# A fused adaLN, attention and MLP kernel: scale, shift and biases made as rows and turned; ScalarE's order by blocks; the second block turned row tile by row tile

## The chip, the core and the metric

The kernel runs on one core of a Trainium2 chip. The metric is the device time of one execution in microseconds (us). The time before is 1591.86 us, the median of three runs from 1589.67 to 1594.28. All times in the text are in us unless marked ns.

The engines are named as in the profile: PE is TensorE (PEld its weight loads), DVE VectorE, ACT ScalarE, POOL GpSimd and SP SyncE, which issues the transfers (DMA). Each engine works through its own list of instructions in order and waits for the others by semaphores. A tile is 128 partitions deep. PE's clock is throttled: the profile shows the clock that was granted, as a share of full speed.

## What is computed

One layer with adaptive layer norm: multi-query attention of 32 heads that share one key and one value head of 16 columns, then an MLP with gelu. All is 32-bit floating point; 2048 rows of 512. Cut to what matters:

```python
mod = (_silu(c) @ w_mod).reshape(c.shape[0], 6, 1, -1)        # c: 1 x 512, w_mod: 512 x 3072
sa, ca, ga, sb, cb, gb = (mod[:, i] for i in range(6))
h = _layernorm(x) * (1 + ca) + sa
q, k, v = h @ wq, h @ wk, h @ wv                              # wq: 512 x 512; wk, wv: 512 x 16
x = x + ga * (softmax(q k^T / 4) v per head) @ wo
h = _layernorm(x) * (1 + cb) + sb
x = x + gb * (gelu(h @ w1 + b1) @ w2 + b2)
```

## The kernel before

The kernel folds the scale `1 + ca` into the weights and turns the shift `sa` into biases: q is (layernorm(x)) times (wq scaled by rows) plus `sa @ wq`, and the keys and values likewise. So before the first product of q it needs the scale as a column (one number for each partition, for each of the four slices of the 512), and before the first q or key leaves PSUM it needs the biases as columns too.

Products that need accuracy are made of three: each operand is split into a high part (rounded) and a low part (the rest), and high by high, low by high and high by low are added up. `split` makes the two parts: the high one on ScalarE or POOL, the low one on VectorE or POOL.

The program has a prologue of some 113 us and then a long regular stretch: 64 units of queries, for each of which PE makes scores (`e`, line 682), ScalarE their exponents, PE the products with the values (`acc`), and VectorE the row maxima (`mx`, line 582) of scores that PE made ahead (`m`, line 577). In that stretch a planner with due times mixes the projections and the MLP in. The change touches the prologue alone; there the order is written out by hand. Every engine's list follows the order of the statements from line 1362 on: what a statement calls goes to the end of each list that it uses.

The rows of x are taken in four blocks of 512 (`xts[0]` to `xts[3]`), each of four row tiles of 128. For a block `stats1` makes mean and variance (VectorE, a power on POOL), `xhat1` normalizes the four row tiles in place (lines 418 and 420; ScalarE, VectorE or POOL), `turn1(b, d)` has PE transpose slice d of the row tiles into one PSUM bank (`tp`, line 428), and `split1(b, d)` splits it: for block 0 a cast on ScalarE and a subtraction on VectorE, for the others a copy on ScalarE (`x`, line 438), a cast on ScalarE (`bigH`, line 140) and a subtraction on POOL (`bigL`, line 145). `keys(b)` makes the 12 products of the block's keys and values (`kps`, line 170), and at the end ScalarE writes the keys (`ks`, line 450); `low_k`, `repeat_k` and `v_out` finish them. `q_group` makes 128 columns of q in 12 products (`qps`). `chunk(n)` is n score products with their maxima, alternating between the two halves of the partitions.

The scale and the shift come from `mod_cols(ps, i, k)`: for slice k of the silu of c it multiplies the 128x128 pieces of `w_mod` (as weights) by one column (`modc`, line 312), 16 products for each of the two. POOL scales the weights of q (`scale_wq`, line 349), and `split_wq` splits them into `wqH` and `wqL` in the order in which the heads are used. The biases of q come from `bias_q` (four products of one column, line 373), `take_col` (a copy on ScalarE, line 377) and `order_q` (a product with the matrix `order`, line 381, that puts the numbers into the heads' order, and a copy on ScalarE). For the first 128 columns this is done ahead, for the other three groups in `prep_wq`, the parts "wq 1" to "wq 3" of the table.

`SLOTS` sets the order of the prologue's later part. Each entry is a slot, and its items are taken from left to right: a number is a `chunk` of so many score products, a name is the next step of that job. "heads b" is `turn1` and `split1` of one slice of block b, "keys b" three key products, "low b" and "k b" the finishing of the keys, "q 1" three products of the second q group, "rows" the four row products of the late modulation (`mod_rows`, `modl`, line 307), which takes the same columns of c 32 times over as weights (`csb`) and data of 512 columns. From slot `WIDE` on, the score products use further banks. `WARM` gives numbers of products that serve nothing but to keep PE busy: `warm_up` at the start, `keep_warm` (`idle`, line 297) elsewhere. After the last slot come nine of these, and then the first scores of the regular stretch.

## Time and profile before

| | |
|---|---|
| runs | 1594.28, 1589.67, 1591.86 us |
| the profiled execution | 1595.28 us, of which the span from the first to the last instruction is 1593.5 us |
| PE busy | 1573.8 us, 99% of the span |
| DVE busy | 1397.7 us, 88% |
| ACT busy | 1230.5 us, 77% |
| POOL busy | 682.1 us, 43% |
| mean granted clock of PE | 0.98 |

How to read the lines that follow. The page cuts the span into 40 equal slices and gives the share of each in tenths. A view by windows has for each window its length, then for each engine its busy time and number of instructions, the granted clock, the share of the DMA engines and the rate. A row of the timeline has start, length, engine, line, operation, output and input tiles, shapes and the number of instructions that follow each other; in brackets stands the idle time ahead of it and what ended it. Such a length runs from the start of the first to the end of the last. A product of unsplit 32-bit operands appears as two instructions of PE, so that 16 such products count as 32; a transpose, or a product of split parts, appears as one. The chain of waits has start, length, engine, tile and line of those pieces that followed from each other up to the last instruction.

### The profile page before, as it was taken

Reading aid. Unit: us, or ns where it says so; the run is one execution under the profiler, and the core shown is the slowest. Engines: PE = TensorE matmul, PEld = TensorE weight load, DVE = VectorE, ACT = ScalarE, POOL = GpSimd, SP = SyncE. Lnnn points to the kernel's source line nnn. Section 1 sums busy time; section 2 is a strip of 40 time slices with the busy share of each in tenths; the row PEclk is TensorE's granted clock in tenths of the full one; section 3 lists DMA queues with packets and bytes.
Section 4 is the critical chain, followed back from the end, with each engine's and each line's share of the span. In section 5 each row is a group of like instructions: output and inputs, shape, how many; then the busy total and the mean of one; then the engine's idle time right before and its main releaser. Section 6 shows DMA issues by size and latency. Waiting matters only on the chain.

```text
span 1593.5 us, 41812 instructions
## 1 busy us (share of the span) xinstructions
PE 1573.8 (99%) x16531; PEld 988.4 (62%) x16531; DVE 1397.7 (88%) x2489; ACT 1230.5 (77%) x2409; POOL 682.1 (43%) x1211
## 2 busy tenths in 40 slices
...
PEclk7679999999999999999999999999999999999999
...
GB/s 207 104 19 121 185 136 45 97 111 60 82 26 103 19 106 33 50 78 56 83 25 103 18 107 32 50 81 49 100 32 76 40 118 26 80 29 98 47 147 47
DMA packets 83976, 120.67 MB, mean 76 GB/s; under 512 B 21294, under 2 KB 56686, under 8 KB 83524
## 3 DMA queue, kind: packets, MB, share of 16 engines
...
q8 instruction: 131, 2.15, 0.6%
...
q10 hardware_dynamic: 16, 0.00, 0.0%
...
## 4 chain that ended last, share of the span: by engine, by line
PE 89%; DVE 8%; DMA 1%; POOL 1%; ACT 1%; SPq 0%; issue 0%; ACTq 0%; DVEq 0%; POOLq 0%
PE acc L703 30%; PE m L577 25%; PE e L682 16%; PE w1ps L203 8%; DVE mx L582 6%; PE w2ps L203 2%; PE w2ps L193 2%; PE w1ps L193 1%; PE kps L170 1%; PE qps L203 1%; PE wops L203 1%; PE tp L203 1%; PE qps L170 0%; PE tp L428 0%; DVE st L888 0%; DMA wml<-in_w_mod_dram 0%
## 5 line engine op out<-in xcount | busy, mean ns | idle before, releaser
L582 DVE TENSOR_REDUCE mx<-m 128x1 f32<-128x512 f32 x2048 | 1270.9, 682 | 113.4 <-PE m L577 92.7
L686 ACT ACTIVATE p<-e 128x512 f32<-128x512 f32 x2048 | 1099.0, 598 | 255.1 <-PE e L682 109.8
L577 PE MATMUL m<-ks,qst 64*128 64x512 f32 x2048 | 838.1, 433 | 5.5 <-DVE ks L454 2.0
L682 PE MATMUL e<-qst,ks 64*128 64x512 f32 x2048 | 740.1, 411 | 0.0
L703 PE MATMUL acc<-p,va 128*32 128x256 f32 x8192 | 548.0, 385 | 0.0
L577 PEld LDWEIGHTS m<-ks,qst 64*128 64x128 f32 x2048 | 368.1, 186 | 209.3 <-DVE mx L582 171.7
L682 PEld LDWEIGHTS e<-qst,ks 64*128 64x128 f32 x2048 | 359.3, 184 | 89.4 <-ACT p L686 62.1
L703 PEld LDWEIGHTS acc<-p,va 128*32 128x32 f32 x8192 | 213.9, 109 | 214.2 <-issue 111.1
L203 PE MATMUL w1ps<-h2H,w1t 64*128 64x256 f32 x1232 | 236.0, 288 | 0.0
L625 POOL TENSOR_SCALAR mt<-turned 8x32 f32<-8x32 f32 x256 | 53.2, 208 | 406.1 <-DVE turned L631 394.2
L203 PEld LDWEIGHTS w1ps<-h2H,w1t 64*128 64x128 f32 x1232 | 185.9, 185 | 29.0 <-issue 21.8
L203 PE MATMUL w1ps<-h2L,w1t 64*128 64x256 f32 x616 | 169.1, 274 | 0.0
L203 PE MATMUL w2ps<-w2H,gH 64*128 64x512 f32 x274 | 120.3, 439 | 0.0
L203 PEld LDWEIGHTS w1ps<-h2L,w1t 64*128 64x128 f32 x616 | 113.9, 185 | 0.0
L203 PE MATMUL w2ps<-w2L,gH 64*128 64x512 f32 x274 | 107.4, 392 | 0.0
L203 PE MATMUL w2ps<-w2H,gL 64*128 64x512 f32 x274 | 106.9, 390 | 0.0
L1040 POOL TENSOR_SCALAR tt<-tt 128x256 f32<-128x256 f32 x77 | 31.0, 403 | 128.4 <-ACT tt L1039 93.5
L1041 POOL TENSOR_TENSOR tt<-tt,z 128x256 f32<-128x256 f32 x77 | 57.0, 740 | 6.4
L145 POOL TENSOR_TENSOR gL<-z,gH 128x256 fp32r<-128x256 f32 x77 | 56.9, 739 | 6.4
L1051 POOL TENSOR_TENSOR z<-tt,z 128x256 f32<-128x256 f32 x77 | 56.4, 732 | 6.0
L1050 POOL TENSOR_TENSOR tt<-tt,z 128x256 f32<-128x256 f32 x77 | 56.9, 739 | 0.0
L203 PEld LDWEIGHTS w2ps<-w2H,gH 64*128 64x128 f32 x274 | 50.4, 184 | 6.7 <-issue 2.9
(216 smaller groups left out, 1573.8 us busy)
## 6 DMA issues: line engine op xcount, KB each, us to landing
...
```

Of the source, the lines that this page charges most:

```text
L145: eng_l.tensor_tensor(out=dst_l, in0=src, in1=raw(dst_h), op=ALU.subtract)
L193: nc.tensor.matmul(ps, a, b_, start=first_, stop=last_)
L203: ins = nc.tensor.matmul(ps, a[rows], b_[rows], start=first_ and s == 0, stop=last_ and s == 1)
L577: nc.tensor.matmul(m, qsts[u][rows, j, t * P:(t + 1) * P], ks[rows, kc * 512:(kc + 1) * 512], start=True, stop=True)
L582: nc.vector.tensor_reduce(out=self.mx[u][:, i, kc:kc + 1], in_=m, axis=AX.X, op=ALU.max)
L625: nc.gpsimd.tensor_scalar(out=mt[:, g:g + 32], in0=turned[g:g + 4 * T, :], scalar1=1.0, scalar2=0.0, op0=ALU.mult, op1=ALU.add)
L682: nc.tensor.matmul(e, ks[rows, kt * P:(kt + 1) * P], rhs, start=True, stop=True)
L686: ins = nc.scalar.activation(dst, e, AF.Exp, scale=0.25)
L703: ins = nc.tensor.matmul(accs[u][32 * cidx:32 * cidx + 32, :], va[:, kt, :], rhs, start=kt == 0, stop=kt == NKT - 1)
L1041: nc.gpsimd.tensor_tensor(out=tt, in0=tt, in1=z, op=ALU.mult)
L1050: nc.gpsimd.tensor_tensor(out=tt, in0=tt, in1=z, op=ALU.mult)
L1051: nc.gpsimd.tensor_tensor(out=z, in0=tt, in1=z, op=ALU.add)
```

## The change

1. *Scale and shift as rows.* `mod_row(ps, i, k)` takes the columns of c, 32 times over, as weights and a 128x512 piece of `w_mod` as data, so that one product replaces four; four of them add up a row of 512 numbers on 32 partitions. ScalarE copies the row from PSUM (`modr`), `turn_rows` transposes its four pieces on PE, and the numbers are read off as columns. For the scale this stands before block 0's turns; for the shift, one row product stands behind each row tile of block 0, and the copy behind the last.
2. *The first weights of q are scaled on ScalarE*, in four instructions, instead of one on POOL.
3. *Biases as rows.* The shift is copied 32 wide (`sab`); `bias_row` multiplies it (as weights) by the unscaled weights of q or of keys and values (as data, 128 columns). ScalarE copies the rows, and puts the heads into order on the way, so that the matrix `order` and its products go; PE turns them. `bias_rest` makes the biases of the other three groups in one go (384 columns of data) in the middle of block 1, and `prep_wq` loses them.
4. *ScalarE's order by blocks.* Blocks 2 and 3 were normalized right behind block 1; now this stands in the slots as "x 2" and "x 3", behind the splits of block 1.
5. *Block 1 is turned row tile by row tile.* Behind each row tile that ScalarE normalizes, PE turns its first three slices and makes two idle products; the fourth slice follows behind the first split. The slots "heads 1" go.
6. `WARM` is (20, 6, 2, 9) for (20, 4, 4, 9); the second number stands once, the third now four times. `WIDE` is 16 for 18, and the slots are laid anew.

The same number of score products is made up to the first exponent; the order of SP's transfers is the same.

```diff
@@ -22,14 +22,13 @@
 LEAD = 6
 LEAD_0 = 6
 FIRST_MAX = ((0, 0), (1, 0), (0, 1), (1, 1), (0, 2), (0, 3), (1, 2), (1, 3))
-SLOTS = (("heads 1", "heads 1"), (2, "heads 1"), (2, "heads 1"),
-         (2, "keys 1"), (2, "keys 1"), (2, "keys 1"), (2, "keys 1"),
-         ("heads 2", "low 1", "k 1", "heads 2"), (2, "heads 2"), (2, "heads 2", "v 0"), (2, "heads 3"),
-         (2, "keys 2"), (2, "keys 2", "heads 3"), (2, "keys 2"), (2, "keys 2"),
-         ("heads 3", "low 2", "k 2", "heads 3"), (2, "wq 1", "keys 3"), (2, "v 1", "keys 3"), (4, "keys 3", "keys 3"),
+SLOTS = ((2, "x 2"), (2, "keys 1"), (2, "keys 1"), (2, "keys 1"), (2, "x 3", "keys 1"),
+         ("heads 2", "low 1", "k 1", "heads 2"), (2, "heads 2"), (2, "heads 2", "v 0"),
+         (2, "heads 3"), (2, "keys 2", "heads 3"), (2, "keys 2"), (2, "keys 2"), (2, "keys 2"), ("heads 3", "low 2", "k 2", "heads 3"),
+         (2, "wq 1", "keys 3"), (2, "v 1", "keys 3"), (4, "keys 3", "keys 3"),
          ("q 1", "low 3", "k 3", "q 1"), (4, "q 1", "v 2", "q 1"), ("wq 2", "v 3"), (4, "rows"),
          (2, "rows"), (2, "rows", "wq 3"), (2, "rows", "load"), (2,))
-WIDE = 18
+WIDE = 16
 MAX_WAIT = (1, 4)
 QBUFS = 4
 PREP = 4
@@ -45,7 +44,7 @@
 SOON = 6
 GROUP = 4
 NORM_WAIT = 6
-WARM = (20, 4, 4, 9)
+WARM = (20, 6, 2, 9)
 MOD_WAIT = 3
 AHEAD = 4.5
 
@@ -306,16 +305,20 @@
         for i, part in enumerate(wm):
             nc.tensor.matmul(ps[32 * i:32 * i + 32, :], csb[:, k, :], part, start=k == 0, stop=k == KD - 1)
 
-    def mod_cols(ps, i, k):
-
-        for d in range(KD):
-            nc.tensor.matmul(ps[:, d:d + 1], wms[k][:, i, d * P:(d + 1) * P], cs[:, k:k + 1], start=k + d == 0, stop=k + d == 2 * KD - 2)
+    def mod_row(ps, i, k):
+
+        nc.tensor.matmul(ps[32 * i:32 * i + 32, :], csb[:, k, :], wms[k][:, i, :], start=k == 0, stop=k == KD - 1)
+
+    def turn_rows(ps, rows, i, n):
+        for k in range(n):
+            nc.tensor.transpose(ps[:, k, :], rows[32 * i:32 * i + 32, k * P:(k + 1) * P], ident[32 * i:32 * i + 32, 32 * i:32 * i + 32])
 
...
     wkL = pro.tile([P, KD, P], F32R, name="wkL")
+    sab = pro.tile([P, KD, 32], F32, name="sab")
     wk0 = pro.tile([P, KD, P], F32, name="wk0")
-    wkm = pro.tile([P, KD, P], F32, name="wkm")
+    wkm = pro.tile([P, KD, P], F32, name="wkm", tag="h32", bufs=4)
...
@@ -328,10 +331,6 @@
...
-
-    order = pro.tile([P, P], F32, name="order")
-    nc.gpsimd.tensor_scalar(out=order.rearrange("p (a r j) -> p a j r", j=2, r=16), in0=ident.rearrange("p (a j r) -> p a j r", j=2, r=16),
-                            scalar1=1.0, scalar2=0.0, op0=ALU.mult, op1=ALU.add)
 
@@ -368,25 +367,29 @@
             nc.scalar.copy(dh, src)
             nc.gpsimd.tensor_tensor(out=dl, in0=src, in1=raw(dh), op=ALU.subtract)
 
-    def bias_q(ps, g):
+    def bias_row(ps, w):
         for k in range(KD):
-            nc.tensor.matmul(ps, wqf[:, k, g * P:(g + 1) * P], sa[:, k:k + 1], start=k == 0, stop=k == KD - 1)
-
-    def take_col(src, g):
-        col = pro.tile([P, 1], F32, name=f"bqn{g}", tag="bqn", bufs=2)
-        nc.scalar.copy(col, src)
-        return col
-
-    def order_q(col, ps, g):
-        nc.tensor.matmul(ps, order, col, start=True, stop=True)
-        nc.scalar.copy(bq[:, g:g + 1], ps)
+            nc.tensor.matmul(ps, sab[:, k, :], w[:, k, :], start=k == 0, stop=k == KD - 1)
+
+    def take_q(dst, ps):
+
+        nc.scalar.copy(dst.rearrange("p (a r j) -> p a j r", j=2, r=16), ps.rearrange("p (a j r) -> p a j r", j=2, r=16))
 
     def prep_wq(g):
         scale_wq(g)
-        ps = psum.tile([P, 2], F32, name=f"bq{g}", **ebank())
-        bias_q(ps[:, 0:1], g)
-        order_q(take_col(ps[:, 0:1], g), ps[:, 1:2], g)
         split_wq(g)
+
+    def bias_rest():
+
+        n = KD - 1
+        ps = psum.tile([P, n * P], F32, name="bqs", tag="x")
+        row = pro.tile([32, n * P], F32, name="bqr", tag="h32", bufs=4)
+        bias_row(ps[:32], wqf[:, :, P:D])
+        for i in range(n):
+            take_q(row[:, i * P:(i + 1) * P], ps[:32, i * P:(i + 1) * P])
+        for i in range(n):
+            nc.tensor.transpose(ps[:, i * P:i * P + 32], row[:, i * P:(i + 1) * P], ident[:32, :32])
+        nc.scalar.copy(bq[:, 1:KD], ps.rearrange("p (i n) -> p i n", n=P)[:, :, 0])
 
     hts = {}
     hts_stats = {}
@@ -1362,35 +1365,45 @@
     warm_up(WARM[0])
     key_rows()
     stats1(0)
-    ps = psum.tile([P, KD], F32, name="modc", tag="x")
+    modr = pro.tile([P, D], F32, name="modr", tag="h32", bufs=4)
+    psr = psum.tile([P, D], F32, name="modrow", tag="x")
+    psc = psum.tile([P, 2, KD, 32], F32, name="modc", tag="v")
     for k in range(KD):
-        mod_cols(ps, 1, k)
-    nc.scalar.activation(ca1, ps, AF.Identity, bias=1.0)
-    scale_wq(0)
-    ps = psum.tile([P, KD], F32, name="modc", tag="v")
+        mod_row(psr, 1, k)
+    nc.scalar.copy(modr[32:64], psr[32:64])
+    turn_rows(psc[:, 1], modr, 1, KD)
+    nc.scalar.activation(ca1, psc[:, 1, :, 0], AF.Identity, bias=1.0)
+    wqms[0] = pro.tile([P, KD, P], F32, name="wqm0", tag="wqm", bufs=1)
+    for k in range(KD):
+        nc.scalar.activation(wqms[0][:, k, :], wqf[:, k, 0:P], AF.Identity, scale=ca1[:, k:k + 1])
     split_wq(0)
     for t, _ in enumerate(xhat1(0, dve)):
         for d in range(KD):
             turn1(0, d, [t])
-        mod_cols(ps, 0, t)
+        mod_row(psr, 0, t)
+    nc.scalar.copy(modr[0:32], psr[0:32])
+    turn_rows(psc[:, 0], modr, 0, KD)
     spread_wkv()
     scaled(wkm, wk0, dve)
     load_constants()
-    nc.vector.tensor_copy(out=sa, in_=ps)
+    nc.vector.tensor_copy(out=sab, in_=psc[:, 0, :, 0:1].to_broadcast([P, KD, 32]))
     for d in range(KD):
         split1(0, d)
     group = q_group()
     run(group, 1)
-    ps = psum.tile([P, 3], F32, name="biases", tag="m", bufs=3)
-    bias_q(ps[:, 1:2], 0)
-    for k in range(KD):
-        nc.tensor.matmul(ps[:, 0:1], wk0[:, k, :], sa[:, k:k + 1], start=k == 0, stop=k == KD - 1)
-    col = take_col(ps[:, 1:2], 0)
+    psb = psum.tile([P, 4, P], F32, name="biases", tag="m", bufs=3)
+    rowb = pro.tile([32, 2, P], F32, name="rowb")
+    bias_row(psb[:32, 0, :], wqf[:, :, 0:P])
+    bias_row(psb[:32, 1, :], wk0)
+    take_q(rowb[:, 0, :], psb[:32, 0, :])
+    nc.scalar.copy(rowb[:, 1, :], psb[:32, 1, :])
     split(wkH, wkL, wkm, act, pool)
-    nc.vector.tensor_copy(out=vbias, in_=ps[:, 0:1])
-    nc.vector.scalar_tensor_tensor(out=kbias, in0=ps[:, 0:1], scalar=kkeep, in1=kmin, op0=ALU.mult, op1=ALU.add)
     run(group, KD - 2)
-    order_q(col, ps[:, 2:3], 0)
+    for i in range(2):
+        nc.tensor.transpose(psb[:, 2 + i, :32], rowb[:, i, :], ident[:32, :32])
+    nc.vector.tensor_copy(out=bq[:, 0:1], in_=psb[:, 2, 0:1])
+    nc.vector.tensor_copy(out=vbias, in_=psb[:, 3, 0:1])
+    nc.vector.scalar_tensor_tensor(out=kbias, in0=psb[:, 3, 0:1], scalar=kkeep, in1=kmin, op0=ALU.mult, op1=ALU.add)
 
     def first_q(t):
         if t == 1:
@@ -1410,17 +1423,24 @@
             repeat_k(0)
 
     stats1(2, first_k)
-    run(xhat1(1, act))
     load_mods(0)
     load_mods(1)
     keep_warm(WARM[1], tag="x", bufs=1)
-    chunk(4)
-    keep_warm(WARM[2], tag="x", bufs=1)
+    for t, _ in enumerate(xhat1(1, act)):
+        if t < 2:
+            chunk(2)
+        for d in range(KD - 1):
+            turn1(1, d, [t])
+        keep_warm(WARM[2], tag="x", bufs=1)
+    split1(1, 0)
+    turn1(1, KD - 1)
+    split1(1, 1)
+    bias_rest()
     stats1(3)
     load_mods(2)
-    run(xhat1(2, act))
-    run(xhat1(3, act, 2))
-    work = {"keys 1": keys(1), "heads 1": heads(1), "heads 2": heads(2), "heads 3": heads(3), "q 1": q_group(), "keys 2": keys(2), "keys 3": keys(3),
+    split1(1, 2)
+    split1(1, 3)
+    work = {"keys 1": keys(1), "x 2": one(run, xhat1(2, act)), "x 3": one(run, xhat1(3, act, 2)), "heads 2": heads(2), "heads 3": heads(3), "q 1": q_group(), "keys 2": keys(2), "keys 3": keys(3),
...
```

How the lists change at the three places of which the prediction speaks. First PE's list at the start, before, from behind `warm_up` to behind the first row tile of block 0 (`modc` is the bank for scale or shift, `wm` a piece of `w_mod`, `tp` a bank of transposes):

```order
L312 MATMUL modc<-cs,wm_133 128x1 x4
L312 MATMUL modc<-cs,wm_134 128x1 x4
L312 MATMUL modc<-cs,wm_135 128x1 x4
L312 MATMUL modc<-cs,wm_136 128x1 x4
L428 MATMUL tp_0_270<-ident,xt_131 128x128
L428 MATMUL tp_1_272<-ident,xt_131 128x128
L428 MATMUL tp_2_274<-ident,xt_131 128x128
L428 MATMUL tp_3_276<-ident,xt_131 128x128
L312 MATMUL modc<-cs,wm_133 128x1 x4
```

and of the change:

```order
L310 MATMUL modrow<-wm_133,csb 32x512
L310 MATMUL modrow<-wm_134,csb 32x512
L310 MATMUL modrow<-wm_135,csb 32x512
L310 MATMUL modrow<-wm_136,csb 32x512
L314 MATMUL modc<-ident,modr 128x32 x4
L431 MATMUL tp_0_266<-ident,xt_131 128x128
L431 MATMUL tp_1_268<-ident,xt_131 128x128
L431 MATMUL tp_2_270<-ident,xt_131 128x128
L431 MATMUL tp_3_272<-ident,xt_131 128x128
L310 MATMUL modrow<-wm_133,csb 32x512
```

Where sixteen products of one column stood (and four behind each row tile), four of 512 columns now stand (and one), with four turns behind the first set.

Then ScalarE's list from the finished keys of block 0 to the keys of block 1 (`xt` a block being normalized, `x` and `bigH` the copy and the cast of a slice), before:

```order
L418 ACTIVATE xt_150<-xt_150,nm_382,rs 128x512 x4
L418 ACTIVATE xt_152<-xt_152,nm_423,rs 128x512 x4
L418 ACTIVATE xt_154<-xt_154,nm_475,rs 128x512 x2
L438 COPY x_1_0_493<-tp_0_488 128x512
L140 CAST bigH<-x_1_0_493 128x512
L438 COPY x_1_1_502<-tp_1_497 128x512
L140 CAST bigH<-x_1_1_502 128x512
L438 COPY x_1_2_517<-tp_2_512 128x512
L140 CAST bigH<-x_1_2_517 128x512
L438 COPY x_1_3_532<-tp_3_527 128x512
L140 CAST bigH<-x_1_3_532 128x512
L450 ACTIVATE ks<-kps_543,cols 128x512
```

and of the change, from behind the scaling of block 1 to just ahead of the keys:

```order
L441 COPY x_1_0_476<-tp_0_440 128x512
L139 CAST bigH<-x_1_0_476 128x512
L441 COPY x_1_1_485<-tp_1_442 128x512
L139 CAST bigH<-x_1_1_485 128x512
L376 COPY bqr<-bqs 32x4x2x16 x3
L392 COPY cols<-bqs 128x3
L441 COPY x_1_2_521<-tp_2_444 128x512
L139 CAST bigH<-x_1_2_521 128x512
L441 COPY x_1_3_525<-tp_3_480 128x512
L139 CAST bigH<-x_1_3_525 128x512
L421 ACTIVATE xt_152<-xt_152,nm_414,rs 128x512 x4
L421 ACTIVATE xt_154<-xt_154,nm_516,rs 128x512 x2
```

The scalings of blocks 2 and 3 moved from ahead of block 1's copies and casts to behind them, and the copies of the three late biases, which wait for PE, stand in the middle.

Last PE's list where the second group of q is made ready (`m` score products, `kps` keys of block 3), before:

```order
L577 MATMUL m_1_1_1_0_719<-ks,qst_158 128x512
L577 MATMUL m_1_1_1_1_722<-ks,qst_158 128x512
L373 MATMUL bq_727<-sa,wqf 128x1 x4
L381 MATMUL bq_727<-bqn_732,order 128x1
L170 MATMUL kps_740<-bigH,wkH 128x512
L170 MATMUL kps_740<-bigH,wkL 128x512
L170 MATMUL kps_740<-bigL,wkH 128x512
```

and of the change:

```order
L580 MATMUL m_1_0_1_0_726<-ks,qst_158 128x512
L580 MATMUL m_1_0_1_1_729<-ks,qst_158 128x512
L169 MATMUL kps_738<-bigH,wkH 128x512
L169 MATMUL kps_738<-bigH,wkL 128x512
L169 MATMUL kps_738<-bigL,wkH 128x512
L580 MATMUL m_1_1_1_0_742<-ks,qst_158 128x512
L580 MATMUL m_1_1_1_1_745<-ks,qst_158 128x512
L476 MATMUL vps_748<-ident,vt_593 128x32 x4
```

The column bias (`bq`) and the product that ordered it are gone from between the score products and the keys.

## The prediction

> **What bounds the kernel now.** I read the page's slices first. The granted clock of TensorE is short of full in the first slices alone (40 us each), so I then cut the first 114 us at the places where the clock changes.
>
> ```profile
> PEclk7679999999999999999999999999999999999999
> ```
>
> ```profile
> core 0: us, PE busy (x) PEld busy (x) DVE busy (x) ACT busy (x) POOL busy (x), PEclk, DMA share, GB/s
> 4.95:11.78 6.83, 6.60 (x61) 6.52 (x59) 3.52 (x11) 0.17 (x1) 1.44 (x7) 1.00 1.12 349
> 11.78:32.26 20.48, 20.48 (x82) 18.71 (x83) 8.64 (x17) 4.32 (x10) 4.06 (x5) 0.50 0.66 219
> 32.26:39.08 6.82, 4.57 (x21) 3.06 (x19) 5.74 (x19) 3.85 (x6) 1.42 (x3) 1.00 0.33 107
> 39.08:45.92 6.84, 6.13 (x19) 4.18 (x19) 6.14 (x15) 4.56 (x7) 2.62 (x6) 0.50 0.83 307
> 45.92:49.32 3.40, 1.57 (x9) 0.80 (x8) 1.71 (x3) 3.13 (x5) 3.40 (x3) 1.00 0.01 2
> 49.32:59.56 10.24, 9.28 (x23) 4.91 (x22) 5.16 (x8) 3.21 (x7) 5.84 (x5) 0.50 0.32 104
> 59.56:62.98 3.42, 2.33 (x15) 1.37 (x13) 1.98 (x3) 3.31 (x6) 1.27 (x1) 1.00 0.00 0
> 62.98:73.22 10.24, 10.24 (x34) 5.86 (x33) 5.30 (x9) 4.92 (x11) 5.01 (x4) 0.50 0.31 102
> 73.22:80.04 6.82, 4.53 (x28) 3.20 (x26) 4.61 (x7) 5.03 (x9) 2.54 (x2) 1.00 0.00 1
> 80.04:86.88 6.84, 6.77 (x20) 4.03 (x21) 2.36 (x4) 1.13 (x5) 3.71 (x4) 0.50 0.00 0
> 86.88:103.94 17.06, 13.68 (x82) 7.75 (x80) 9.89 (x18) 4.79 (x12) 6.36 (x12) 1.00 0.09 32
> 103.94:114.18 10.24, 9.29 (x30) 4.84 (x32) 3.77 (x6) 1.63 (x5) 1.66 (x3) 0.50 0.09 19
> 114.18:1593.50 1479.32, 1475.15 (x16116) 920.08 (x16113) 1337.45 (x2368) 1188.94 (x2330) 638.49 (x1136) 1.00 0.23 73
> ```
>
> From 114.18 us on PE is busy 1475.15 of 1479.32 us at full clock, and no instruction there is changed. Whatever the change does happens before that. There the half-clock stretches (rows with 0.50) sum to 20.48 + 6.84 + 10.24 + 10.24 + 6.84 + 10.24 = 64.9 us, and PE is busy in most of each: the prologue is bound by PE at half speed. The rises stand at 32.26, 45.92, 59.56, 73.22, 86.88 and 114.18: 13.66 us apart, or twice that. The clock falls after a thin stretch, on steps of 3.41 us, and then waits for the next of those rises however busy PE is (10.24 of 10.24 us at 0.50 before 73.22).
>
> Last, the chain of waits in order of time and the timeline give landmarks and durations.
>
> ```profile
> 12.89 1.50 PE modc L312 x8
> 46.10 4.12 POOL xt L420 x2
> 55.34 1.58 PE kps L170 x3
> 59.25 0.69 ACT ks L450
> 74.56 0.92 PE kps L170 x3
> 75.50 0.45 ACT ks L450
> 88.15 0.79 ACT ks L450
> 108.96 4.21 PE idle L297 x9
> 113.17 0.72 PE e L682 x2
> ```
>
> ```profile
> 7.87 3.68 PE L312 MATMUL modc<-cs,wm 128*128 128x1 f32 x32
> 19.16 1.09 PE L428 MATMUL tp<-ident,xt 128*128 128x128 f32 x4
> 21.61 0.78 PE L170 MATMUL qps<-h0H,wqH 128*128 128x512 f32 x1
> 34.96 0.78 ACT L450 ACTIVATE ks<-kps,cols 128x512 fp32r<-128x512 f32 x1
> 35.75 0.68 ACT L459 ACTIVATE vt<-kps,cols 32x512 f32<-32x512 f32 x1
> 37.24 0.62 ACT L463 CAST ks<-ks 16x512 fp32r<-16x512 f32 x1 [0.81 <-DVE ks L454]
> 37.89 5.75 ACT L418 ACTIVATE xt<-xt,nm,rs 128x512 f32<-128x512 f32 x8
> 47.68 0.58 ACT L438 COPY x<-tp 128x512 f32<-128x512 f32 x1
> 48.30 0.62 ACT L140 CAST bigH<-x 128x512 fp32r<-128x512 f32 x1
> 49.44 1.29 DVE L582 TENSOR_REDUCE mx<-m 128x1 f32<-128x512 f32 x2 [1.63 <-PE m L577]
> 75.30 1.04 PE L428 MATMUL tp<-ident,xt 128*128 128x128 f32 x8
> 76.69 1.05 PE L373 MATMUL bq<-sa,wqf 128*128 128x1 f32 x8
> 80.11 0.59 PE L381 MATMUL bq<-bqn,order 128*128 128x1 f32 x2 [2.36 <-ACT bqn L377]
> 95.87 1.06 PE L307 MATMUL modl<-wml,csb 128*32 128x512 f32 x8
> 103.79 0.48 PE L381 MATMUL bq<-bqn,order 128*128 128x1 f32 x2 [2.22 <-ACT bqn L377]
> 104.92 1.93 PE L307 MATMUL modl<-wml,csb 128*32 128x512 f32 x8
> ```
>
> The landmarks are: the first q product at 21.61, the keys of blocks 0 to 3 leaving ScalarE at 34.96, 59.25, 75.50 and 88.15, the first exponent's product at 113.17. A group of three key products takes 1.58 at half and 0.92 at full clock. The clock fell at 11.78 right after 3.68 us of one-column products, which count PE busy but stream next to nothing; I read them as its cause.
>
> **The change, stage by stage, first at full clock.** No row shows a row product (32 columns of weights, 512 of data) alone: modl runs four of them side by side in 1.06 (full) or 1.93 (half). One alone costs between a quarter (0.27, 0.48) and the whole (1.06, 1.93). All four go to one strip, so I take nearly the whole: 0.9 and 1.75.
>
> *To the first q product.* Four row products, 3.6, replace the 3.68. Added in series on ScalarE and PE: the copy 0.58, four turns at 1.04 / 8 = 0.13 and handoffs, some 1.4, so block 0's turns start near 12.9 where they started at 11.8. The four scalings moved from POOL to ScalarE are off this path, since the weights' split is not read until the q products. Then four times a row tile (0.52) and a row product (0.9): 5.7; the second copy 0.58 and the first cast 0.62: the q product starts near 19.9, against 21.61. At half clock the loop is 4 x (1.0 + 1.75) = 11 and it starts near 25.4.
>
> *To the first keys* (13.35 before, at half clock until 32.26). Eight groups of three at about 0.8, 6.4; eight 128-column row products, a quarter of 0.9 each, 1.8 (half clock 3.5, where the one-column ones took as much); the rest is waits for the bias copies. About 9: keys at 28.8, gained so far 6.2.
>
> *To the second keys* (24.29 before). There POOL's 4.12 us of scaling block 3 stood ahead of block 1's split; now it stands behind. ScalarE's queue now sets the stage: 2.93 to the first scaling as before (34.96 to 37.89); four scalings at 5.75 / 8 = 0.72, 2.9; PE's last row tile and the idle products between tiles 1.5; two copy-and-cast pairs 2 x 1.2; then a wait for four 384-column bias products (0.68 each at full clock, 2.7 of which 1.3 is covered by that second pair): 1.4; three bias copies, turns and the column copy 1.6 (bounds for a copy: 0.15 as a column, 0.58 at full length); two more pairs 2.4; six scalings 4.3. Sum 19.4: keys at 48.2, gained 11. Behind the wait stand the scalings of blocks 2 and 3, so at half clock everything later is late with it.
>
> *To the third keys* (16.25 before, 10.24 of it at half clock). Until then ScalarE has six copy-and-cast pairs, 7.2, and the key and value copies, 0.78 + 0.62 + 0.68; with PE's own waits some 11 where these sum to 9.3. Gained 16.2.
>
> *To the fourth* (12.65). The column bias step is gone: 1.05 + 0.59 and the 2.36 for which PE waited on ScalarE, 4.0. Gained 20.2.
>
> *To the first exponent* (25.02). Two more such steps go: 1.05 + 0.48 + 2.22 = 3.75 for the last; the other lies between 1.64 with no wait and the 4.0 of the first, and I take 2. At full clock the nine idle products take 2.1 for 4.21, and modl 0.9 less. One pair of maxima more lands here: 1.29. Net 7.4, in all 27.6.
>
> *At no cost* I count three edits. SP's order of transfers is the same in both programs; the loads for the late rows wait for block 1's transposes, which only come earlier. The matrix that ordered the bias columns was made on POOL before anything waited for POOL. The column `sa` becomes a copy 32 wide on VectorE ahead of the four splits of block 0: up to half a copy's length, 0.3, which the second turn of the rows leaves idle on PE anyway; were it not hidden, the first q products would be 0.3 later.
>
> **What the clock takes back.** Three places of the new order are thin. (i) After the six idle products PE has two score products and some transposes in 2.5 us while the keys are finished (a stretch like 32.26:39.08, after which it fell): even odds, price 2.7 for the bias products and 3 for row tiles and idles, 2.9 in the mean. (ii) Between second and third keys PE waits for ScalarE's copies, as in 59.56:62.98: a fall nearly sure, on average half of 13.66 us long, which is two thirds of the 10.24 in that stage before and so of its 5.2: 3.5. (iii) Before the end PE goes at VectorE's pace of 1.29 a pair: 1.5. Handoffs that I left out, some 2. Taken back: 10. Gain 17.6.
>
> The profiled execution took 1595.28 us, span 1593.5 and 1.78 around it; it becomes 1577.7. It lies 3.4 above the median of the runs, 1591.86, so the forecast is **1574**.
>
> The Trainium skill (TensorE: Matmul & The Clock Gate, Part 1: The HAM clock gate) states that the clock comes back after one busy window of about 3.4 us, free-running. On the step of the falls the trace agrees; its rises, 13.66 apart, do not bear the rule out, and an estimate by the page would shorten each half-clock stretch to a window or so.
>
> **Rivals.**
> 1. *The clock returns at any 3.41 us step when work is dense.* Then each half-clock stretch lasts about a quarter of 13.66. The three falls then cost about 3 in all, gain 24: 1568. Against it: 10.24 us stretches in which PE never paused. 0.10. This is what the page of the Trainium skill named above states.
> 2. *Row products on one strip do not hold the clock*, since they fill a quarter of the array. It falls at 11.78 as before: the q product near 25.4 (+3.8), later stages as slow as before, and only the three bias steps (4.0 + 5.75, less the 1.29) are won: 8.5 - 3.8 = 4.7, 1587. For it: no row shows one strip alone. Against: modl's stretch kept full clock. 0.15.
> 3. *ScalarE or VectorE takes over as the bound* from the second keys on; PE's shorter waits only move to them. VectorE was busy 9.89 of 17.06 in 86.88:103.94, ScalarE 5.03 of 6.82, so there is room; gain 2, 1590. 0.07.
> 4. *Slower: block 1's row tiles miss the rises.* Transposes with short idles between them are too thin when a rise is due, so the two before 59.56 are missed and ScalarE stands at the bias products (4 x 1.3 at half clock, 5.2) with blocks 2 and 3 behind it. Each missed rise costs about 6.8 us of the 13.66; it decides once two are missed: 13.6 against the 8.4 of the bias steps, +5: 1597. For it: 39.08:45.92 was of this kind; against: it did rise after it. 0.11.
>
> **How the numbers follow.** The forecast has 0.57, its own range 1564 to 1584. What a measurement can tell from no change is 0.3%, 4.8 us. Faster by more: forecast, rival 1 and some 0.6 of rival 2, 0.76. Within it: the rest of rival 2, rival 3 and a little of rival 4, 0.14. Slower: 0.10. The range runs from 1564 (clock lost for short stretches only) to 1589, into rival 2.
>
> **What would show it.** Cut at the clock's changes, the new profile should show 1.00 from about 5 us to at least 29; the first q product before 20.5; first keys near 29, second near 48 to 54, fourth before 75, the first exponent between 86 and 103; bqs products with ScalarE idle under 2 us before bqr. A 0.50 row starting near 11.8 is rival 2; second keys after 60 is rival 4; a gap between the rises other than 13.66 is rival 1. If the stretch after the first exponent is not 1479 us long, the place of the whole argument is wrong.

## The result, and the profile after

The changed kernel took 1573.98 us (median; 1571.72 to 1576.97), beside it the kernel before 1590.76: the ratio is 0.9896, 95% interval 0.9867 to 0.9925. It was measured once more together with the last three experiments: 1576.6 (1573.9 to 1578.29) against 1590.34, ratio 0.9907, 0.9890 to 0.9924. All nine runs of the changed kernel have the median 1574.09. The forecast was 1574, range 1564 to 1589. The profiled execution took 1574.09 us, span 1572.3; forecast for it was 1577.7.

The clock in the page's slices, of the kernel after (one digit for 1/40 of the span):

```profile
PEclk9999999999999999999999999999999999999999
```

The first three slices, 7, 6 and 7 before, are now 9, which stands for 90% or more. Cut where the clock changes, and at the first exponent, the same profile gives (columns as in the prediction: us, busy us and count of PE, PEld, DVE, ACT, POOL, granted clock, DMA share, GB/s). The first row starts at 4.95, where the clock rose in the kernel before; here it rose at 4.81.

```profile
core 0: us, PE busy (x) PEld busy (x) DVE busy (x) ACT busy (x) POOL busy (x), PEclk, DMA share, GB/s
4.95:52.60 47.65, 42.82 (x207) 24.59 (x205) 31.54 (x73) 26.16 (x50) 18.64 (x26) 1.00 0.66 225
52.60:59.42 6.82, 6.74 (x20) 3.86 (x20) 3.74 (x6) 4.72 (x10) 5.48 (x5) 0.50 0.47 155
59.42:79.90 20.48, 16.59 (x80) 9.07 (x79) 14.73 (x24) 9.32 (x19) 8.15 (x9) 1.00 0.07 26
79.90:86.74 6.84, 6.60 (x25) 1.45 (x29) 2.98 (x6) 0.19 (x2) 2.44 (x8) 0.50 0.01 2
86.74:91.52 4.78, 3.87 (x24) 2.11 (x16) 4.33 (x8) 0.72 (x2) 3.18 (x6) 1.00 0.09 22
91.52:1572.30 1480.78, 1476.21 (x16119) 920.33 (x16118) 1337.79 (x2369) 1189.44 (x2331) 638.44 (x1136) 1.00 0.23 73
```

and the kernel before from its own first exponent on:

```profile
113.10:1593.50 1480.40, 1476.23 (x16119) 920.87 (x16118) 1337.45 (x2368) 1189.78 (x2331) 638.49 (x1136) 1.00 0.23 73
```

From the first exponent on the two programs take the same time, 1480.78 and 1480.40. All of the 21.2 us between the profiled executions was won before it. There the half-clock time went from 64.9 us to 6.82 + 6.84 = 13.7; the clock stood at 1.00 from its first rise to 52.60, where it used to fall at 11.78.

The landmarks, from the timeline of the kernel after (start, us, engine, line, operation, out<-in, idle before and what ended it in brackets):

```profile
20.01 0.50 PE L169 MATMUL qps<-h0H,wqH 128*128 128x512 f32 x1
29.32 0.78 ACT L453 ACTIVATE ks<-kps,cols 128x512 fp32r<-128x512 f32 x1
48.18 0.78 ACT L453 ACTIVATE ks<-kps,cols 128x512 fp32r<-128x512 f32 x1
62.38 0.78 ACT L453 ACTIVATE ks<-kps,cols 128x512 fp32r<-128x512 f32 x1 [3.55 <-PE kps L169]
70.01 0.78 ACT L453 ACTIVATE ks<-kps,cols 128x512 fp32r<-128x512 f32 x1
91.52 0.59 PE L685 MATMUL e<-qst,ks 64*128 64x512 f32 x2
```

Against 21.61, 34.96, 59.25, 75.50, 88.15 and 113.10 the gains are 1.6, 5.6, 11.1, 13.1, 18.1 and 21.6 us.

The parts that the prediction had to bound stand in the same timeline:

```profile
7.89 3.62 PE L310 MATMUL modrow<-wm,csb 128*32 128x512 f32 x8
11.55 0.58 ACT L1373 COPY modr<-modrow 32x512 f32<-32x512 f32 x1 [8.36 <-PE modrow L310]
12.18 0.43 PE L314 MATMUL modc<-ident,modr 32*128 32x32 f32 x4 [0.67 <-ACT modr L1373]
...
37.74 2.77 PE L372 MATMUL bqs<-wqf,sab 128*32 128x384 f32 x8
...
40.55 0.58 ACT L376 COPY bqr<-bqs 32x128 f32<-32x128 f32 x3 [1.66 <-PE bqs L372]
...
41.58 0.16 ACT L392 COPY cols<-bqs 128x3 f32<-128x3 f32 x1 [0.46 <-PE bqs L391]
```

One row product on one strip is 3.62 / 4 = 0.905 us at full clock (two records each, x8), where 0.9 was taken. ScalarE waited 1.66 for the bias products (1.4 forecast).

Last, what stands at the second fall of the clock, at 79.90:

```profile
79.27 0.72 ACT L367 CAST wqH<-wqm 128x256 fp32r<-128x256 f32 x2 [2.38 <-POOL wqm L348]
...
79.89 0.20 ACT L477 COPY va<-vps 128x64 f32<-128x64 f32 x1
...
80.14 0.79 PE L580 MATMUL m<-ks,qst 64*128 64x512 f32 x1 [2.18 <-ACT va L477]
80.86 1.93 PE L306 MATMUL modl<-wml,csb 128*32 128x512 f32 x8
```

PE waits 2.18 us for the copy of block 3's values `va`, which frees a bank; the copy stands on ScalarE behind the cast of the third group's weights (`"wq 2"` ahead of `"v 3"` in the slots), and that cast waited 2.38 for POOL. While PE waits the clock falls, and the next group of four `modl` products takes 1.93 for 1.06. The prediction expected a fall before the end, but from VectorE's pace.

### The profile page after: what moved, and what is told of

The parts are those of the page before. It is cut to its first block, busy times and chain, and to the rows that moved or that the text cites. A ratio compares the mean times of both kernels' runs of the same rounds, so it can differ in the third digit from the quotient of the medians.

```text
span 1572.3 us, 41712 instructions
## 1 busy us (share of the span) xinstructions
PE 1556.0 (99%) x16478; PEld 964.5 (61%) x16478; DVE 1396.5 (89%) x2490; ACT 1232.0 (78%) x2413; POOL 680.6 (43%) x1209
## 4 chain that ended last, share of the span: by engine, by line
PE 87%; DVE 7%; DMA 0%; issue 0%; DVEq 0%; ACT 0%; SPq 0%
PE acc L706 30%; PE m L580 25%; PE e L685 16%; PE w1ps L202 8%; DVE mx L585 6%; PE w2ps L202 2%; PE w2ps L192 2%; PE qps L202 1%; PE w1ps L192 1%; PE wops L202 1%; PE tp L202 1%; DVE st L891 0%; PE wops L192 0%; DVE x L884 0%; PE modl L306 0%; DMA qst<-ml 0%
## 5 line engine op out<-in xcount | busy, mean ns | idle before, releaser
L685 PEld LDWEIGHTS e<-qst,ks 64*128 64x128 f32 x2048 | 359.1, 184 | 90.0 <-ACT p L689 62.8
```

What stands on the lines that cost most here:

```text
L685: nc.tensor.matmul(e, ks[rows, kt * P:(kt + 1) * P], rhs, start=True, stop=True)
```

## The experiments

The question was what held the clock, what rows and order bring apart, and whether the rises really come on a grid of 13.66 us. Every kernel was timed beside the kernel before, in as many executions as the table says; the landmarks are from one profiled execution each.

| kernel | median us (range, runs) | ratio [95%] | clock first rises | first q | keys 0 / 1 / 2 / 3 | first exponent | half clock, first 125 us |
|---|---|---|---|---|---|---|---|
| before | 1590.3 to 1592.4 in four batches | 1 | 4.95 | 21.61 | 34.96 / 59.25 / 75.50 / 88.15 | 113.10 | 64.9 |
| after | 1573.98 (1571.72–1576.97, 4) | 0.9896 [0.9867, 0.9925] | 4.81 | 20.01 | 29.32 / 48.18 / 62.38 / 70.01 | 91.52 | 13.7 |
| after_again | 1576.60 (1573.90–1578.29, 5) | 0.9907 [0.9890, 0.9924] | 6.00 | 20.57 | 29.88 / 52.46 / 64.14 / 71.77 | 94.18 | 23.9 |
| cols_back | 1578.14 (1572.88–1579.52, 6) | 0.9909 [0.9894, 0.9925] | 4.78 | 21.43 | 32.14 / 53.89 / 66.83 / 74.47 | 96.08 | 30.7 |
| cols_fed | 1588.36 (1580.54–1589.29, 12) | 0.9970 [0.9958, 0.9982] | 6.53 | 31.00 | 42.84 / 63.16 / 77.50 / 85.14 | 106.74 | 41.0 |
| cols_full | 1583.22 (1578.25–1592.97, 12) | 0.9945 [0.9926, 0.9964] | 6.34 | 34.62 | 46.27 / 66.57 / 80.87 / 88.50 | 110.06 | 41.0 |
| order_only | 1583.37 (1579.92–1588.14, 6) | 0.9946 [0.9928, 0.9964] | 7.08 | 20.80 | 33.94 / 53.51 / 65.17 / 78.77 | 105.38 | 51.2 |
| rows_only | 1583.98 (1582.19–1587.89, 6) | 0.9953 [0.9937, 0.9970] | 7.47 | 21.27 | 30.57 / 58.94 / 73.70 / 81.33 | 104.37 | 34.1 |
| late_cols | 1580.59 (1578.64–1583.82, 6) | 0.9934 [0.9919, 0.9948] | 8.03 | 21.54 | 30.83 / 48.26 / 62.31 / 75.91 | 100.53 | 27.3 |
| no_idle | 1574.47 (1572.60–1577.11, 5) | 0.9891 [0.9874, 0.9908] | 6.13 | 20.64 | 29.93 / 50.05 / 61.52 / 69.16 | 91.06 | 13.7 |
| pool_scale | 1575.07 (1573.60–1576.74, 4) | 0.9899 [0.9878, 0.9920] | 7.49 | 21.29 | 30.59 / 50.87 / 65.07 / 72.70 | 94.15 | 17.1 |
| v_first | 1570.46 (1569.00–1573.11, 4) | 0.9866 [0.9849, 0.9884] | 7.92 | 21.48 | 30.78 / 51.09 / 65.39 / 73.02 | 89.40 | 13.7 |
| v_wq1 | 1569.18 (1566.89–1569.53, 4) | 0.9861 [0.9844, 0.9879] | 5.70 | 20.42 | 29.69 / 48.58 / 62.96 / 69.43 | 85.19 | 10.2 |
| filled | 1567.17 (1564.46–1570.14, 4) | 0.9852 [0.9831, 0.9874] | 7.17 | 21.13 | 30.44 / 52.57 / 65.36 / 71.81 | 86.83 | 10.2 |

The clock's first rise is listed because every later change of the clock lies a multiple of 3.41 us behind it, and because it comes at another time in each execution, 4.78 to 8.03. It alone moves the first q product of the changed kernel from 20.01 (rise at 4.81) to 21.48 (rise at 7.92) with the same instructions up to there. Landmarks of two profiles are therefore compared as differences from one landmark to the next.

**cols_back: do the one-column products cost the clock?** The changed kernel with scale and shift as single columns, all else kept:

```diff
     for k in range(KD):
-        mod_row(psr, 1, k)
-    nc.scalar.copy(modr[32:64], psr[32:64])
-    turn_rows(psc[:, 1], modr, 1, KD)
+        mod_cols(ps, 1, k)
...
-        mod_row(psr, 0, t)
-    nc.scalar.copy(modr[0:32], psr[0:32])
-    turn_rows(psc[:, 0], modr, 0, KD)
+        mod_cols(ps, 0, t)
```

> The change with scale and shift made as one-column products again (no row products, copies and turns for these two; biases still as rows). Clock theory: the clock falls near 11.8 as in the kernel before and rises at 32.3 at the latest, the first q product near 21.6 (20.0 in the change), keys of block 0 near 34 (29.3); total 1574 + 4 to 6 = 1578 to 1580. Rival (row products only shorten PE's list, the clock follows other things): PE's list is no longer and two copies and turns leave the path, so 1572 to 1574, and the clock stays up past 11.8.

Measured 1578.14. From the windows of cols_back, cut at the clock's changes:

```profile
4.78:11.61 6.83, 6.66 (x61) 6.57 (x60) 3.56 (x12) 0.15 (x1) 1.46 (x7) 1.00 1.10 343
11.61:25.26 13.65, 13.65 (x61) 12.26 (x62) 5.11 (x12) 4.08 (x11) 1.99 (x3) 0.50 0.80 279
```

The fall right after the one-column products is back (11.61; 11.78 in the kernel before), although PE counted busy for 6.66 of the 6.83 us ahead of it; at 11.6 the changed kernel is at full speed. What this is worth in time is less clear. By the medians it is 4 us (1578.1 against 1574.1), by the means of these six runs and the nine of the changed kernel 2, and the ranges overlap (1572.88 to 1579.52 and 1571.72 to 1578.29), as do the intervals of the ratio. So the fall is shown, and a gain from the rows of scale and shift alone is likely but not shown.

**cols_fed and cols_full: is it the share of time in which columns stream?** Single columns again, with a row product whose result is not used ahead of each four; 256 columns long in cols_fed, 512 in cols_full:

```diff
+    def feed(ps, i, k):
+
+        nc.tensor.matmul(ps[32 * i:32 * i + 32, 0:D // 2], csb[:, k, :], wms[k][:, i, 0:D // 2], start=True, stop=True)
...
     for k in range(KD):
+        feed(fed, 1, k)
         mod_cols(ps, 1, k)
```

> As the kernel with one-column products again, plus eight row products of 256 columns whose result nobody reads, one ahead of each slice's columns: the same results by the same columns, and more work on PE (8 x 0.45 us). Clock theory: the stream keeps the clock up past 11.8; keys of block 0 near 31, total 1575 to 1577, faster than without the extra work. Rival (it is the length of PE's list): 3.6 us slower than without the extra work, 1582.

> Scale and shift as single columns again, with one full row product of 512 columns (result unused) ahead of each group of four single columns, so that TensorE streams about half of each 1.82 us, where the half-length ones streamed a third and lost the clock at 13.35. Theory (what holds the clock is the share of time in which columns stream): no fall before 25 us, first q product at 24 to 27, first keys at 34 to 37, 1578 to 1583 us, faster than the half-length feed (1588.4) although it adds work. Rival (any group of single columns loses the clock, or a half is too little): fall between 11 and 15, first q product after 30, 1589 to 1596 us.

Both texts on cols_fed missed: 1588.36. The feed did not hold the clock. From the timeline of cols_fed, and from that of cols_full:

```profile
8.71 0.62 PE L319 MATMUL fed<-wm,csb 128*32 128x256 f32 x2
9.26 1.05 PE L315 MATMUL modc<-cs,wm 128*128 128x1 f32 x8
```

```profile
8.62 1.05 PE L319 MATMUL fed<-wm,csb 128*32 128x512 f32 x2
9.60 1.05 PE L315 MATMUL modc<-cs,wm 128*128 128x1 f32 x8
```

The next pair starts at 10.25 in the first and 10.58 in the second, 1.54 and 1.96 us later. With 0.905 for the 512 columns of a row product, columns stream in about 0.45 of 1.54 (29%) and 0.9 of 1.96 (46%). Their windows, cols_fed:

```profile
6.53:13.35 6.82, 6.82 (x51) 5.42 (x51) 5.21 (x16) 0.00 (x0) 1.04 (x1) 1.00 1.12 348
13.35:37.24 23.89, 23.89 (x88) 16.47 (x88) 3.43 (x7) 4.96 (x14) 1.46 (x3) 0.50 0.48 159
```

and cols_full:

```profile
6.34:16.59 10.25, 10.25 (x63) 6.73 (x63) 5.27 (x16) 0.03 (x1) 1.04 (x1) 1.00 1.09 358
16.59:40.48 23.89, 23.89 (x76) 13.96 (x75) 3.37 (x6) 4.56 (x14) 1.46 (x3) 0.50 0.34 110
```

PE is busy without a gap in all four rows, and in both programs the clock falls and stays down for seven steps. But this execution is the longest of the twelve of cols_full. Six of the twelve took 1578.25 to 1581.43 us at a mean clock of 0.996 to 0.998; 0.998 leaves some (1 - 0.998) x 1577 / 0.5 = 6 us of half clock where the profiled run has 41. Of cols_fed, with less work, one run of twelve came below 1585, at 0.994. So by the mean clock alone, since no execution that kept the clock was profiled, a share near 46% goes with a kept clock in about half of the executions and one near 29% in one of twelve. That PE is busy is not enough to keep the clock; that the share of streaming decides is argued from these two feeds and cols_back, and the share at which the clock is lost stays open. The expectation for cols_full (no fall before 25) failed in the profiled run, and the mean clock of the lower six speaks for it there.

All 14 traces together tell how far busy time does decide. Each was cut into steps of 3.41 us from the clock's first rise to 125 us. At full clock there are 364 such steps. PE was busy for less than 0.64 of the step in 27, and the clock fell at the end of all 27; for 0.64 to 0.85 in 77, and it fell after 19; for more than 0.85 in 260, and it fell after 5. These bounds are read from the same steps. The five lie in the one-column stretches of before, cols_back, cols_fed, cols_full and order_only, one in each, with PE busy for 0.93 to 1.00 of them. So outside such a stretch a step that was well filled never lost the clock in these traces. At half clock PE was busy for 0.93 or more in each of the 51 steps that end in a rise, but also in 54 of the 64 that do not.

**order_only and rows_only: which half brings what?** order_only is the kernel before with the slots, the idle products and block 1's row tile by row tile order of the change; rows_only is the change with the slots, idle products and order of the kernel before, the late biases ahead of the slots.

```diff
-    run(xhat1(1, act))
...
-    chunk(4)
-    keep_warm(WARM[2], tag="x", bufs=1)
+    for t, _ in enumerate(xhat1(1, act)):
+        if t < 2:
+            chunk(2)
+        for d in range(KD - 1):
+            turn1(1, d, [t])
+        keep_warm(WARM[2], tag="x", bufs=1)
```

> The kernel before with ScalarE's order by blocks, block 1 row tile by row tile, the new slots and idle products, but all of scale, shift and biases as columns. Theory: clock low from 11.8 to 32.3, keys of block 0 near 35; second keys near 52 to 55 (59.3 before) since POOL's 4 us of scaling no longer stands ahead of block 1's split; the three bias steps still stop PE for 2 us each; 1582 to 1587. Rival (the order is worth nothing without the rows): 1590 to 1593.

> The kernel before with the rows (scale, shift and biases as rows and turned; the late biases in one group ahead of the slots) but with its own order of blocks, slots and idle products. Order alone gave 9 us (1592.4 to 1583.4). If rows and order simply add up to the 17 of the whole change, 1583 to 1585 us, first exponent near 104. If the rows carry most of it, since they hold the clock from the start, 1576 to 1581 us, first exponent 94 to 100. In both cases TensorE keeps full clock from 5 us to past the first keys (near 29 to 31 us).

order_only won 1592.38 - 1583.37 = 9.0 us, rows_only 1592.33 - 1583.98 = 8.4: together 17.4, where the whole change won 16.8 and 13.7 in its two batches. They add up within the spread, by the first of the two texts on rows_only, so each half has its gain without the other. The order shows between first and second keys, where the kernel before takes 24.29: 53.51 - 33.94 = 19.57 in order_only, 58.94 - 30.57 = 28.37 in rows_only, whose ScalarE again scales blocks 2 and 3 ahead of block 1's copies. The rows show where the order cannot: from the third keys to the first exponent the kernel before takes 37.6 us, order_only 40.2, rows_only 30.7 and the changed kernel 29.1. The clock's first fall is no part of what the order wins. The windows of order_only show it again behind the one-column products, and five steps at half clock with PE busy throughout:

```profile
7.08:13.91 6.83, 6.83 (x64) 6.83 (x63) 5.63 (x15) 0.17 (x1) 2.15 (x2) 1.00 1.11 344
13.91:30.98 17.07, 17.07 (x69) 15.40 (x68) 5.20 (x12) 4.23 (x10) 3.34 (x5) 0.50 0.64 210
```

**late_cols: the biases of the later groups.** The changed kernel with `bias_rest` taken out and the column product, its ordering product and two copies back in the slots of `wq`:

```diff
     def prep_wq(g):
         scale_wq(g)
+        ps = psum.tile([P, 2], F32, name=f"bq{g}", **ebank())
+        bias_q(ps[:, 0:1], g)
+        order_q(take_col(ps[:, 0:1], g), ps[:, 1:2], g)
         split_wq(g)
...
-    bias_rest()
```

> The change with the three late biases of q made as columns in the slots again (bias_rest gone, the rest as rows). Theory: ScalarE gets 3 us back in block 1 (second keys near 45), each of the three steps stops PE 1.6 to 4 us later on, and one-column products let the clock fall: 1574 + 5 = 1577 to 1582. Rival (the waits of PE only moved to ScalarE's wait for the rows): 1573 to 1575.

Measured 1580.59, 6.5 more than the nine runs of the change. Second keys near 45 missed, since they came at 48.26. They came 17.43 after the first. The changed kernel, without a fall of the clock in that stage, has 18.86, and v_first, with a fall of one step at 35, has 20.31. late_cols had that fall (35.33), so the bias rows cost 20.31 - 17.43 = 2.9 us there. From third to fourth keys 13.60 took the place of 7.63, from there to the first exponent 24.62 that of 21.51. The trade is 2.9 us on ScalarE's path early for 6.0 + 3.1 later.

**no_idle: the idle products between row tiles.**

```diff
-WARM = (20, 6, 2, 9)
+WARM = (20, 6, 0, 9)
```

> The changed kernel without the two idle products after each of block 1's four row tiles (the six ahead of them stay). Theory: those products hold the clock while ScalarE sets the pace; without them it falls between 35 and 46 us and the bias products and row tiles run at half clock: 3 to 6 us longer than the changed kernel, 1577 to 1580 us, second keys at 50 to 55. Rival: the row tiles and the bias products of 384 columns are dense enough alone: 1572 to 1575 us, second keys near 47.5.

1574.47: the rival. From the windows of no_idle:

```profile
33.44:40.27 6.83, 6.30 (x21) 3.88 (x22) 6.26 (x19) 4.64 (x8) 3.09 (x5) 0.50 0.88 308
40.27:70.99 30.72, 26.71 (x122) 15.02 (x121) 22.48 (x35) 22.15 (x42) 21.33 (x19) 1.00 0.21 71
```

The clock does fall, two steps long, but second keys come 20.12 after the first, within 0.2 of v_first and pool_scale, which have the idles and a fall of one step. The stage goes at ScalarE's pace, and the eight idles can go. This profile also has no fall between second and third keys: 11.47 us, against 14.20 in the changed kernel, 14.30 in v_first and 14.20 in pool_scale, which lose two steps there. That is the price of the fall at 52.60: 2.7.

**pool_scale: the scaling that moved from POOL to ScalarE.**

```diff
-    wqms[0] = pro.tile([P, KD, P], F32, name="wqm0", tag="wqm", bufs=1)
-    for k in range(KD):
-        nc.scalar.activation(wqms[0][:, k, :], wqf[:, k, 0:P], AF.Identity, scale=ca1[:, k:k + 1])
+    scale_wq(0)
```

> The changed kernel with the first group's weights scaled by POOL as before, not by ScalarE in four pieces. The prediction counted this edit at nothing, since the first q products come after the copy of the rows and the cast on ScalarE in any case. By that: 1573 to 1575 us, first q product 20 to 21.5. Rival: POOL's scaling, after its other work, holds up the split of the weights and so the first q products by 1 us or more: 1575.5 to 1577 us, first q product after 22.

1575.07, first q product at 21.29 with the first rise at 7.49; v_first, which has the scaling on ScalarE, has 21.48 at 7.92. The edit is worth nothing that can be measured, as counted.

**v_first: the wait before the end.**

```diff
-("wq 2", "v 3")
+("v 3", "wq 2")
```

> Slot 21 turns block 3's values ahead of the weights of the third head group, not behind them. Theory: TensorE's wait of 2.18 us at 80.14 in the changed kernel goes, since ScalarE no longer stands at POOL's scaling of the weights (2.38) ahead of the copy that frees the bank; with it goes the clock's fall at 79.9, so the maxima before the end are no longer held up by modl products of 1.93 us: 2 to 4.5 us less than the changed kernel, 1569.5 to 1572 us, first exponent at 87 to 89.5. Rival: the stage goes at VectorE's pace of maxima in any case and the fall costs nothing there: 1573 to 1575 us, first exponent near 91.

1570.46. From the timeline of v_first, and below it from its windows:

```profile
79.80 0.20 ACT L477 COPY va<-vps 128x64 f32<-128x64 f32 x1
...
80.47 0.50 PE L580 MATMUL m<-ks,qst 64*128 64x512 f32 x2
80.89 1.06 PE L306 MATMUL modl<-wml,csb 128*32 128x512 f32 x8
...
82.28 0.75 ACT L367 CAST wqH<-wqm 128x256 fp32r<-128x256 f32 x2 [2.27 <-POOL wqm L348]
...
89.40 0.59 PE L685 MATMUL e<-qst,ks 64*128 64x512 f32 x2
```

```profile
62.53:89.40 26.87, 24.11 (x125) 12.19 (x124) 21.50 (x36) 10.30 (x21) 12.72 (x20) 1.00 0.06 22
```

ScalarE waits for POOL as before (2.27), but nobody waits for ScalarE there: no bracket stands behind the score products, `modl` takes 1.06, and the clock stays at 1.00. From fourth keys to first exponent 16.38 takes the place of 21.51: 5.1 us for the wait and the fall together, which no run separates. It does not rest on one execution. The eight profiles that have `"wq 2"` ahead of `"v 3"` and the late biases as rows (after, after_again, cols_back, cols_fed, cols_full, rows_only, no_idle, pool_scale) all have half clock in this stage and take 21.4 to 23.0; the three with the two names swapped have none and take 15.0 to 16.4. The time of the whole gains less than the stage: v_first also loses a step behind the first exponent (93.25 to 96.67), and its half clock sums to the same 13.7.

**v_wq1 and filled: can the rest be had?** v_wq1 also makes the second group's weights while POOL stands idle during block 2's keys. filled adds idle products in the two thin places, ten for six after the first keys and two in each of two slots.

```diff
-         (2, "heads 3"), (2, "keys 2", "heads 3"), (2, "keys 2"), (2, "keys 2"), (2, "keys 2"), ("heads 3", "low 2", "k 2", "heads 3"),
-         (2, "wq 1", "keys 3"), (2, "v 1", "keys 3"), (4, "keys 3", "keys 3"),
+         (2, "heads 3"), (2, "keys 2", "heads 3"), (2, "wq 1", "keys 2"), (2, "keys 2"), (2, "keys 2"), ("heads 3", "low 2", "k 2", "heads 3"),
+         (2, "keys 3"), (2, "v 1", "keys 3"), (4, "keys 3", "keys 3"),
```

```diff
-         ("heads 2", "low 1", "k 1", "heads 2"), (2, "heads 2"), (2, "heads 2", "v 0"),
+         ("heads 2", "low 1", "k 1", "heads 2"), (2, "idle", "heads 2"), (2, "idle", "heads 2", "v 0"),
...
-WARM = (20, 6, 2, 9)
+WARM = (20, 10, 2, 9)
...
+            elif part == "idle":
+                keep_warm(2, tag="x", bufs=1)
```

> Block 3's values ahead of the third group's weights, and the second group's weights made two slots of block 2's keys earlier, while POOL stands idle for 4.2 us. Theory: ScalarE's wait of 2.40 us for POOL at 69.29, and with it TensorE's 1.25 and the 2 us by which block 3's keys leave late, go: fourth keys 1.5 to 2.5 us sooner after the third than in the changed kernel (7.63 there), 0.5 to 1.5 us less than with the swap alone: 1569 to 1570 us. Rival: the maxima at VectorE's pace before the end take it back: 1570.5 us, no change from the swap alone.

> As the one above, and idle products where the clock fell: ten in place of six after block 0's keys, and two in each of the two slots of maxima that follow block 1's keys. Theory: the falls at 33 to 36 and at 52 to 56 us, 3.4 and 6.8 us at half clock, go; the idles lie where TensorE waits for ScalarE and VectorE. No half clock between 8 and 85 us, 1.5 to 3.5 us less than without them: 1566 to 1568 us. Rival: ScalarE sets the pace there and half clock costs nothing, or the idles push the transposes back as much: 1569 to 1571 us.

v_wq1: 1569.18. Its timeline:

```profile
60.53 1.04 POOL L348 TENSOR_TENSOR wqm<-wqf,ca 128x512 f32<-128x512 f32 x1
61.60 0.73 ACT L367 CAST wqH<-wqm 128x256 fp32r<-128x256 f32 x2 [2.38 <-POOL wqm L348]
...
69.43 0.78 ACT L453 ACTIVATE ks<-kps,cols 128x512 fp32r<-128x512 f32 x1 [1.84 <-PE kps L169]
```

ScalarE's wait of 2.4 us now lies in time that it spent waiting for PE's key products in any case. Fourth keys follow the third by 6.47 for 7.63, 1.2 us sooner (1.5 to 2.5 expected), and then wait for PE. The gain over v_first, 1.3 us, is within the spread of the runs.

filled: 1567.17. Its windows:

```profile
7.17:44.72 37.55, 34.18 (x158) 19.32 (x158) 23.28 (x61) 17.30 (x37) 11.09 (x17) 1.00 0.78 261
44.72:54.96 10.24, 10.24 (x29) 5.62 (x27) 5.51 (x9) 6.92 (x11) 6.24 (x5) 0.50 0.00 1
54.96:86.83 31.87, 31.03 (x163) 16.90 (x162) 27.85 (x46) 17.15 (x34) 19.37 (x24) 1.00 0.15 51
86.83:1567.80 1480.97, 1476.26 (x16119) 920.72 (x16118) 1337.72 (x2369) 1189.41 (x2331) 639.18 (x1139) 1.00 0.23 73
```

The falls at 33 to 36 and 52 to 56 are absent here, which one execution does not put down to the idles, and the clock fell at 44.72, behind the wait for the bias rows: "no half clock between 8 and 85" was wrong. Two of the four runs show a mean clock of 1.000, and these took 1564.46 and 1564.74; the other two 1569.61 and 1570.14. All four runs of filled and all four of v_wq1 lie below the fastest run of the changed kernel (1571.72), so both beat both kernels. Between these two the runs don't decide.

**after_again: the phase.** The changed kernel, unchanged.

> The changed kernel as it is, on the same chip and beside the same runs of the kernel before as the three below. 1571.5 to 1577 us by its first runs, median near 1574. By phase of the clock's steps it should in some executions lose the clock at 33 to 36 us (as four of the five programs with the same first keys did: 35.33, 35.23, 33.44, 34.78) and in some not (52.60 as the first fall).

Its windows at half clock:

```profile
43.55:53.79 10.24, 10.24 (x27) 5.91 (x26) 5.90 (x10) 6.50 (x10) 6.63 (x4) 0.50 0.01 5
...
74.27:87.92 13.65, 13.31 (x47) 5.11 (x50) 6.83 (x11) 2.74 (x7) 3.79 (x5) 0.50 0.11 40
```

Neither of the two named places: the same program that fell at 52.60 and 79.90 for 13.7 us fell here at 43.55 and 74.27 for 23.9 us and took 1577.2 where it had taken 1574.09. The five runs stand in the order of their mean clock: 0.996 for 1573.90 and 1573.95, 0.995 for 1576.60, 0.992 for 1577.20 and 1578.29. So the spread between runs of one program goes with what the clock loses, and that differs with where its steps fall.

## Why the prediction was right, point by point

- **Place.** Right: nothing changed behind the first exponent (1480.78 and 1480.40), and the half-clock time in the prologue was what could be won.
- **First q product 19.9, first keys 28.8.** Measured 20.01 and 29.32; the row product cost 0.905 against 0.9. Rival 2 (one strip does not hold the clock) fell: 1.00 to 52.60. cols_back shows that without the rows the clock falls at 11.6. The prediction's reading of the one-column products as the cause of that fall holds.
- **Second keys 48.2.** Measured 48.18, no fall on the way. Of (i), "even odds, 2.9": of the six profiles with the changed kernel's list up to there (after, after_again, v_first, v_wq1, pool_scale, late_cols) three fell between 34.8 and 35.4. Three of six fit even odds; the price is mis-sized, 20.31 - 18.86 = 1.4. A fourth, after_again, fell later in the same stage, at 43.55, and there it cost more: 52.46 - 29.88 = 22.58, 3.7 over 18.86. So that the profiled execution had no fall in this stage was luck. The idles put there against it hold nothing that can be measured.
- **Third keys, (ii) "a fall nearly sure, 3.5".** It came at 52.60, 6.82 long. 48.2 + 11.1 + 3.5 = 62.8 was forecast, 62.38 measured. The price was 2.7, and the length of 6.8 was luck (below).
- **Fourth keys.** 8.7 behind the third were forecast, 7.63 measured. No column bias, no wait for one.
- **First exponent.** The step that failed within a forecast that was met. 17.6 at full clock and 1.5 for (iii), 19.1, were forecast; 21.51 measured. (iii) named VectorE's pace; v_first shows that PE's wait for `va` behind `wqH` behind POOL, and the fall after it, cost 5.1, and that without them the stage takes 16.38. The term was mis-sized and its cause was wrong: the swap leaves VectorE's work as it was, so its pace does not need those 5.1; the slots, with "wq 2" ahead of "v 3" before and after, showed the order that makes this wait.
- **"The clock waits for the next of those rises", 13.66 apart.** Wrong, though it changed the sum little. The 51 half-clock stretches in the first 125 us of the 14 profiles last 1 step of 3.41 us in 17 cases, 2 in 19, and 3 to 7 in 15; cols_back rises at 52.57 and 62.81, 10.24 apart. The grid in the kernel before was an accident of one execution. The two stretches of the profile after are 6.8 long, what half of 13.66 gave, by luck: in after_again, the same program, they are 10.24 and 13.65 long.
- **Rival 1** has the step right and not the length: the clock can return at any step, but in 34 of 51 stretches it took more than one, in order_only 17.07 us with PE busy for all of them. The Trainium skill (TensorE: Matmul & The Clock Gate, Part 1: The HAM clock gate) states a free-running window of about 3.4 us that does not start with the kernel, and a return after at least one busy window. On the first the traces agree (first rise 4.78 to 8.03, all changes on steps of 3.41); on the second, 17 of the 51 stretches end after one window, if busy is what the profile calls busy. PE was busy for at least 0.93 of the step before each of the 51 rises, but also in 54 steps that brought none; what else a step must hold to bring the clock back stays open.
- **Rivals 3 and 4** fell: third and fourth keys came 13 and 18 us earlier. ScalarE did set the pace up to the second keys, as the forecast had it, but no other engine took the gain back, and the wait before `bqr` was 1.66 us where rival 4 needed some 5.
- **The sum.** A gain of 17.6 was forecast for the profiled execution, 21.6 measured by the landmarks. (i) did not come in it (2.9), the fall of (ii) and the fourth keys took 0.4 and 1.0 less, the 2 of handoffs cannot be found; the last stage took 2.4 more. 2.9 + 0.4 + 1.0 + 2 - 2.4 = 3.9 of the 4.0. The total was better than its parts, since misses of both signs met in it.
- **Median.** The profiled execution of before lay 3.4 above the median that was shown, that of after at its median. So the forecast for the median, 1574, was met, while that for the profiled execution, 1577.7, was 3.6 too long. That the median was met to the microsecond is luck: 3.6 too long for the profiled execution and 3.4 taken off for a distance that the changed kernel does not show nearly cancel, and the five later runs of the same kernel have the median 1576.6.
